# A smaller warm-up operand, and the last cast of a kernel shared by two engines

## Chip, cores, metric

The kernel runs on one core of one Trainium2 chip. The metric is the device time of one execution in microseconds (us), lower is better. A profile gives the *span*, from the first to the last instruction; here it is about 1.8 us shorter than the device time (318.9 against 320.73 us for the profiled execution of the kernel before).

## The reference

A dense layer with SiLU and its gradients, all in bf16. B=1, S=2048, D=640, F=1536.

```python
def _fwd_reference(x, w1, w2):
    h = jnp.einsum("bsd,df->bsf", x, w1)
    h = _silu(h)
    return jnp.einsum("bsf,fd->bsd", h, w2)

def reference(x, w1, w2, grad_out):          # cut: dtype plumbing
    out, vjp = jax.vjp(_fwd_reference, x, w1, w2)
    return (out, *vjp(grad_out))             # out, gx, gw1, gw2
```

## The kernel before

Two places matter: the first 8 us and the last 4.

**The start.** TensorE has nothing to do until x arrives. It fills the time with matmuls on a tile of ones, meant to have its clock released sooner: in the trace of before, the first products run 213 ns apart until the trace records the release, at 5.66 us, and 109 ns apart after it. These matmuls, and the first loads, are moved ahead of the entry barrier. Then ten PE transposes turn the first rows of x, and `h_first` multiplies them by w1, slice by slice as the slices land.

```python
warm = cpool.tile([P, P], dt_in, name="warm")
early = [nc.vector.memset(warm[:], 1.0)]
...
wp = ps_h.tile([P, SC], FP32, name="wp", tag="hp")
for i in range(NWARM):                                   # NWARM = 18
    early.append(nc.tensor.matmul(wp[:, 0:P], lhsT=warm[:], rhs=warm[:], start=True, stop=True))
...
early += [load_x(nc.sync, 0), load_x(nc.scalar, 1)]
early += [load_w1(0, slice(0, F // 2)), load_w1(0, slice(F // 2, F), nc.scalar)]
early += [load_w1(k) for k in range(1, 3)]
start_before_entry_wait(nc, {i.ins.name for i in early})
...
    # h_first: 12 products for each of the 5 slices (dt_) of w1
    for dt_ in range(DT):
        for pair in range(NPAIR):
            h_pair_mm(hs[0][pair], pair, dt_, xT, halves[0])
    for pair in range(NPAIR):
        pair_silu(hs[0][pair], pair, aT, halves[0])      # ScalarE reads hs[0][pair] in PSUM
        if pair < NCOPY:
            h_sb = hpool.tile([P, 2, HC], FP32, name="h_sb")
            nc.vector.tensor_copy(out=h_sb[:], in_=hs[0][pair][:])   # VectorE reads it too
```

**The end.** The last tile of gw1 (128x512) is computed in two PSUM banks, 384 columns and then 128. Each part is cast to bf16 and stored. Only the cast and the store of the last 128 columns come after the last matmul. `wait_for_last_store_last` makes the closing waits check this store last.

```python
for k, (lo, hi) in enumerate(((0, FC - P), (FC - P, FC))):
    gp = ps_h.tile([P, FC], FP32, name="hp")
    for st in range(ST):
        nc.tensor.matmul(gp[:, lo:hi], lhsT=x_nat[:, st, dt_ * P:(dt_ + 1) * P],
                         rhs=gh_blk[:, st, lo:hi], start=(st == 0), stop=(st == ST - 1))
    g1 = s1pool.tile([P, FC], dt_in, name="g1")          # s1pool has 3 buffers
    if k == 0:
        nc.scalar.activation(g1[:, lo:hi], gp[:, lo:hi], ACT.Copy)
    else:
        nc.vector.tensor_copy(out=g1[:, lo:hi], in_=gp[:, lo:hi])
    last_store = nc.sync.dma_start(
        out=gw1_v[:, dt_, fc * FC + lo:fc * FC + hi], in_=g1[:, lo:hi])
wait_for_last_store_last(nc, last_store.ins.name)
```

The semaphores between engines are not in the source: the framework places them where it sees a conflict between two instructions.

Of the kernel before, what the change touches and what calls it, by code (L numbers as in the profile page):

```python
# [9 lines left out]
ACT = mybir.ActivationFunctionType  # L10
# [32 lines left out]
def wait_for_last_store_last(nc, name):  # L43



    def move(nc):
        blocks = nc.m.functions[0].blocks
        store = next(i for b in blocks for i in b.instructions if i.name == name)
        lanes = {u.id for u in store.sync_info.on_update}  # L50
        end = blocks[-1].instructions
        at = next(k for k, i in enumerate(end) if i.engine == mybir.EngineType.SP)
        waits = list(end[at].sync_info.on_wait)
        late = [w for w in waits if w.id in lanes]
        assert len(late) == 1 and not end[at].sync_info.on_update
        waits = late + [w for w in waits if w.id not in lanes]
        end[at] = copy.replace(end[at], sync_info=mybir.SyncInfo(on_wait=waits, on_update=[]))

    nc.at_finalize(move)
# [3 lines left out]
def kernel(  # L63
# [11 lines left out]
    nc = tc.nc  # L75
    P = 128
# [13 lines left out]
    NFC = F // FC  # L90
    FB = FC // P
    LAG = 2
    NWARM = 18
    HC = 2 * P
    NPAIR = FT // 2
    NCOPY = 4
    dt_in = x.dtype
# [35 lines left out]
    with ExitStack() as mctx:  # L133
        cpool = mctx.enter_context(tc.tile_pool(name="cpool", bufs=1))
# [4 lines left out]
        hpool = mctx.enter_context(tc.tile_pool(name="hpool", bufs=NCOPY))  # L139
        opool = mctx.enter_context(tc.tile_pool(name="opool", bufs=2))  # L140

        warm = cpool.tile([P, P], dt_in, name="warm")
        early = [nc.vector.memset(warm[:], 1.0)]
        warm_a = cpool.tile([P, 1], FP32, name="warm_a")
        wp = ps_h.tile([P, SC], FP32, name="wp", tag="hp")
        for i in range(NWARM):
            early.append(nc.tensor.matmul(wp[:, 0:P], lhsT=warm[:], rhs=warm[:], start=True, stop=True))

        ident = cpool.tile([P, P], dt_in, name="ident")
        make_identity(nc, ident[:])  # L150
# [166 lines left out]
        for c in range(NCH):  # L317
# [15 lines left out]
            if c == 0:  # L333
                h_first(xT, aT, ghT)
                nc.sync.dma_start(
                    out=aT_scr[:, c * SC:(c + 1) * SC].rearrange("(ft p) s -> p ft s", p=P), in_=aT[:]
                )
                sd_phase(c, w2_nat, aT, oT_scr)
                for ft in range(FT):
                    g_group(ft, goT, ghT)  # L340
                nc.sync.dma_start(
                    out=ghT_scr[:, c * SC:(c + 1) * SC].rearrange("(ft p) s -> p ft s", p=P), in_=ghT[:]
# [4 lines left out]
            for i in range(FT + LAG):  # L347
# [7 lines left out]
                out=aT_scr[:, c * SC:(c + 1) * SC].rearrange("(ft p) s -> p ft s", p=P), in_=aT[:]  # L355
            )
            nc.sync.dma_start(
                out=ghT_scr[:, c * SC:(c + 1) * SC].rearrange("(ft p) s -> p ft s", p=P), in_=ghT[:]
# [7 lines left out]
    with ExitStack() as fctx:  # L366
# [18 lines left out]
        for fc in range(NFC):  # L385
            a_blk = a_blks[fc]
            g2T = fpool.tile([P, DT, FC], dt_in, name="g2T")
# [3 lines that stand above are left out]
                    nc.tensor.matmul(  # L391
                        gp[:],
                        lhsT=go_nat[:, st, dt_ * P:(dt_ + 1) * P],
                        rhs=a_blk[:, st, :],
                        start=(st == 0),
                        stop=(st == ST - 1),
# [8 lines left out]
        def store_gw2(fc):  # L405
            g2 = fpool.tile([P, FB, D], dt_in, name="g2")
            nc.sync.dma_start_transpose(out=g2[:], in_=g2T_scr[:, fc * FC:(fc + 1) * FC])
            nc.sync.dma_start(out=gw2_v[:, fc * FB:(fc + 1) * FB, :], in_=g2[:])
# [3 lines left out]
        for fc in range(NFC):  # L412
            gh_blk = gh_blks[fc]
            for dt_ in range(DT):
                if dt_ == DT // 2:
                    store_gw2(fc)
                if fc == NFC - 1 and dt_ == DT - 1:
# [3 lines that stand above are left out]
                            nc.tensor.matmul(  # L421
                                gp[:, lo:hi],
                                lhsT=x_nat[:, st, dt_ * P:(dt_ + 1) * P],
                                rhs=gh_blk[:, st, lo:hi],
                                start=(st == 0),
                                stop=(st == ST - 1),
                            )
                        g1 = s1pool.tile([P, FC], dt_in, name="g1")
                        if k == 0:
                            nc.scalar.activation(g1[:, lo:hi], gp[:, lo:hi], ACT.Copy)  # L430
                        else:
                            nc.vector.tensor_copy(out=g1[:, lo:hi], in_=gp[:, lo:hi])  # L432
                        last_store = nc.sync.dma_start(
                            out=gw1_v[:, dt_, fc * FC + lo:fc * FC + hi], in_=g1[:, lo:hi]
                        )
                    wait_for_last_store_last(nc, last_store.ins.name)
                    continue
                gp = ps_h.tile([P, FC], FP32, name="hp")
                for st in range(ST):
                    nc.tensor.matmul(  # L440
                        gp[:],
                        lhsT=x_nat[:, st, dt_ * P:(dt_ + 1) * P],
                        rhs=gh_blk[:, st, :],
                        start=(st == 0),
                        stop=(st == ST - 1),
                    )
                g1 = s1pool.tile([P, FC], dt_in, name="g1")
                if k % 2 == 0:
                    nc.scalar.activation(g1[:], gp[:], ACT.Copy)
                else:  # L450
                    nc.vector.tensor_copy(out=g1[:], in_=gp[:])  # L451
                k += 1
                nc.sync.dma_start(out=gw1_v[:, dt_, fc * FC:(fc + 1) * FC], in_=g1[:])
# [30 lines left out]
```

## Time and profile before

| | before |
|---|---|
| time, 3 runs ahead of the prediction | 320.31 us (320.27 to 320.48) |
| span of the profiled run | 318.92 us |
| TensorE busy | 314.2 us, 99% |
| end of the last matmul to the issue of the last store | 0.410 us |
| issue of the last store to its landing | 1.455 us |
| its landing to the end of the span | 0.775 us |

The profile page, busy times and the chain of waits (shares of the span by engine):

```profile
PE 314.2 (99%) x1516; PEld 150.7 (47%) x1544; DVE 102.7 (32%) x182; ACT 76.8 (24%) x139; POOL 0.7 (0%) x6
...
PE 96%; DMA 2%; issue 1%; SPq 0%; DVE 0%; DVEq 0%
```

TensorE is the bound from end to end. A change outside it can only act where TensorE does not run yet or no longer runs.

The timeline of the start. Columns: start in us, duration in us, engine, line, operation, tiles, shapes; in brackets the idle time of the engine before it and what ended it.

```profile
0.28 0.17 DVE L143 MEMSET warm<- 128x128 bf16 x1 [0.28 <-issue]
...
0.50 2.10 PE L147 MATMUL wp<-warm 128*128 128x128 bf16 x18 [0.50 <-DVE warm L143]
...
2.59 0.98 PEld L195 LDWEIGHTS <-x_nat 128*128 128x128 bf16 x10 [0.25 <-DMA x_nat<-in_x_dram]
...
6.18 1.21 PEld L233 LDWEIGHTS <-w_nat 128*128 128x128 bf16 x12 [0.30 <-DMA w_nat<-in_w_dram]
...
7.73 0.33 PEld L233 LDWEIGHTS <-w_nat 128*128 128x128 bf16 x4 [0.35 <-DMA w_nat<-in_w_dram]
```

The brackets are the point: after the warm-up, the transposes wait for x, and the products wait for two slices of w1. The chain of waits, in order of time, for the same stretch (start, duration, what), says the same:

```profile
1.47 6.22 DMA w_nat<-in_w_dram
7.69 0.05 issue
7.74 10.65 PE hp L233 x96
```

The end, as chain of waits, and the last matmul and the stores in the timeline (the second line merges two stores; the last one is the final 0.33 us of it, 316.69 to 317.02):

```profile
312.79 3.51 PE hp L421 x32
316.30 0.04 DVEq L432
316.33 0.04 issue
316.38 0.29 DVE g L432
```

```profile
316.06 0.22 PE L421 MATMUL hp<-gh_blk,x_nat 128*128 128x128 bf16 x1
...
315.94 1.08 SPq L433 DMA_DIRECT2D out_dram<-g  x2
```

A cast of 128 columns is thus in series with everything that follows. One more line is from the list of waits between 10 and 12 us: engine, tile and line, what it waited for, total us, times, longest:

```profile
DVE h_sb L266 <- ACT aT L242: 7.1, 1, 7.1
```

VectorE's copy writes `h_sb` and reads PSUM. It uses no result of ScalarE's silu, which only *reads* the same PSUM tile. Still it waited for it.

### The profile page before, as it was taken

How to read it: one execution, taken by the hardware profiler on the slowest of the kernel's cores; microseconds unless marked ns; L12 is line 12 of the kernel's file. 1: busy time of each engine (PE TensorE's matmuls, PEld its weight loads, DVE VectorE, ACT ScalarE, POOL GpSimd, SP SyncE). 2: the span in 40 equal slices, each digit the busy share in tenths (PEclk: the TensorE clock that was granted, in tenths of full speed). 3: DMA queues.
4: the chain of work that ended last, by engine and by line, in shares of the span. 5: the costliest groups of instructions: out<-in, count | busy, mean ns of one | idle time of the engine just before them, and what ended most of it. 6: DMA issues, size and time to landing. Idle time of an engine off the chain costs nothing.

```text
span 318.9 us, 3632 instructions
## 1 busy us (share of the span) xinstructions
PE 314.2 (99%) x1516; PEld 150.7 (47%) x1544; DVE 102.7 (32%) x182; ACT 76.8 (24%) x139; POOL 0.7 (0%) x6
## 2 busy tenths in 40 slices
PE   9999999999999999999999999999999999999996
PEld 7854444444444444444444444444444444444443
DVE  1494641477410187710147741000000100001001
ACT  2691000644201354311064420111100001001100
POOL 0000000000000000000000000000000000000000
PEclk9999999999999999999999999999999999999999
DMA  8999999999999866492544089919999999996111
GB/s 268 311 177 222 216 266 255 313 270 304 260 232 342 201 191 174 144 299 82 164 120 128 0 268 265 210 38 290 222 258 255 228 214 339 229 311 216 38 39 45
DMA packets 147233, 67.02 MB, mean 210 GB/s; under 512 B 113937, under 2 KB 146705, under 8 KB 147217
## 3 DMA queue, kind: packets, MB, share of 16 engines
q1 hardware_dynamic: 146928, 66.43, 83.0%
q10 hardware_dynamic: 288, 0.36, 0.3%
q8 instruction: 12, 0.20, 0.3%
q14 instruction: 5, 0.03, 0.0%
HBM read 9.18 MB, written 28.97 MB: 120 GB/s over the span
## 4 chain that ended last, share of the span: by engine, by line
PE 96%; DMA 2%; issue 1%; SPq 0%; DVE 0%; DVEq 0%
PE hp L302 32%; PE hp L286 16%; PE hp L391 16%; PE hp L440 15%; PE hp L204 12%; PE hp L233 3%; DMA w_nat<-in_w_dram 2%; PE hp L421 1%; SPq L173 0%; SPq L170 0%; DVE g L432 0%; DVEq L432 0%; SPq L468 0%
## 5 line engine op out<-in xcount | busy, mean ns | idle before, releaser
L286 PE MATMUL hp<-goT,w2T 128*128 128x512 bf16 x239 | 56.8, 379 | 0.1
L302 PE MATMUL hp<-ghT,w1T 128*128 128x512 bf16 x235 | 52.2, 379 | 0.3
L302 PE MATMUL hp<-aT,w_nat 128*128 128x512 bf16 x234 | 52.1, 379 | 0.3
L391 PE MATMUL hp<-a_blk,go_nat 128*128 128x512 bf16 x235 | 51.7, 379 | 0.3
L440 PE MATMUL hp<-gh_blk,x_nat 128*128 128x512 bf16 x219 | 48.2, 379 | 0.3
L204 PE MATMUL hp<-xT,w_nat 128*128 128x512 bf16 x174 | 43.4, 379 | 0.3
L310 ACT ACTIVATE oT<-hp 128x512 bf16<-128x512 f32 x24 | 14.5, 604 | 106.8 <-PE hp L302 106.8
L302 PEld LDWEIGHTS <-w1T 128*128 128x128 bf16 x240 | 23.5, 98 | 28.3
L391 PEld LDWEIGHTS <-go_nat 128*128 128x128 bf16 x240 | 23.5, 98 | 28.3
L286 PEld LDWEIGHTS <-w2T 128*128 128x128 bf16 x240 | 23.5, 98 | 28.3
L302 PEld LDWEIGHTS <-w_nat 128*128 128x128 bf16 x240 | 23.5, 98 | 28.1
L293 DVE SCALAR_TENSOR_TENSOR ghT<-ghT,hp 128x512 bf16<-128x512 bf16 x48 | 32.5, 681 | 7.3 <-PE hp L286 7.3
L440 PEld LDWEIGHTS <-x_nat 128*128 128x128 bf16 x224 | 21.9, 98 | 26.4
L312 DVE CAST oT<-hp 128x512 bf16<-128x512 f32 x16 | 11.1, 691 | 72.2 <-PE hp L302 67.7
L213 ACT ACTIVATE aT<-hp 128x512 bf16<-128x512 f32 x36 | 21.5, 597 | 30.4 <-PE hp L204 30.4
L204 PEld LDWEIGHTS <-w_nat 128*128 128x128 bf16 x180 | 17.6, 98 | 21.3
L220 DVE SCALAR_TENSOR_TENSOR ghT<-aT,v 128x512 bf16<-128x512 bf16 x36 | 24.6, 684 | 0.2
L219 DVE TENSOR_SCALAR v<-t 128x512 bf16<-128x512 f32 x36 | 15.4, 426 | 26.7 <-ACT t L217 26.7
L217 ACT ACTIVATE t<-hp 128x512 f32<-128x512 f32 x36 | 21.3, 592 | 0.0
L451 DVE CAST g<-hp 128x512 bf16<-128x512 f32 x7 | 4.8, 691 | 47.0 <-PE hp L440 34.5
L401 DVE CAST g2T<-hp 128x512 bf16<-128x512 f32 x7 | 4.8, 692 | 46.1 <-PE hp L391 46.1
L399 ACT ACTIVATE g2T<-hp 128x512 bf16<-128x512 f32 x8 | 4.8, 597 | 47.0 <-PE hp L391 47.0
(28 smaller groups left out, 77.3 us busy)
## 6 DMA issues: line engine op xcount, KB each, us to landing
aT_scr<-aT SPq DMA_DIRECT2D x4, 1536.0 KB, 6.3
ghT_scr<-ghT SPq DMA_DIRECT2D x4, 1536.0 KB, 8.2
out_dram<-o_sb SPq DMA_DIRECT2D x8, 640.0 KB, 3.3
oT_scr<-oT SPq DMA_DIRECT2D x4, 640.0 KB, 3.6
go_nat<-in_grad_out_dram SPq DMA_DIRECT2D x4, 640.0 KB, 8.3
gxT_scr<-oT SPq DMA_DIRECT2D x4, 640.0 KB, 4.7
w_nat<-in_w_dram SPq DMA_DIRECT2D x1, 1920.0 KB, 11.1
x_nat<-in_x_dram SPq DMA_DIRECT2D x3, 640.0 KB, 7.2
```

Of the source, the lines that this page charges most:

```text
L204: nc.tensor.matmul(hp[:], lhsT=w1_nat[:, dt_, ft * P:(ft + 1) * P], rhs=xT[:, dt_, :], start=(dt_ == 0), stop=(dt_ == DT - 1),)
L213: nc.scalar.activation(aT[:, ft, :], hp[:], ACT.Silu)
L217: nc.scalar.activation(t[:], hp[:], ACT.Tanh, scale=0.5)
L219: nc.vector.tensor_scalar(out=v[:], in0=t[:], scalar1=-0.5, scalar2=0.5, op0=ALU.mult, op1=ALU.add)
L220: nc.vector.scalar_tensor_tensor(out=ghT[:, ft, :], in0=aT[:, ft, :], scalar=1.0, in1=v[:], op0=ALU.subtract, op1=ALU.mult)
L286: nc.tensor.matmul(gp[:], lhsT=w2T[:, dt_, ft * P:(ft + 1) * P], rhs=goT[:, dt_, :], start=(dt_ == 0), stop=(dt_ == DT - 1),)
L293: nc.vector.scalar_tensor_tensor(out=ghT[:, ft, :], in0=ghT[:, ft, :], scalar=1.0, in1=gp[:], op0=ALU.add, op1=ALU.mult)
L302: nc.tensor.matmul(op_[:], lhsT=w_all[:, ft, dt_ * P:(dt_ + 1) * P], rhs=rhs_all[:, ft, :], start=(ft == 0), stop=(ft == FT - 1),)
L310: nc.scalar.activation(oT[:, dt_, :], op_[:], ACT.Copy)
L312: nc.vector.tensor_copy(out=oT[:, dt_, :], in_=op_[:])
L391: nc.tensor.matmul(gp[:], lhsT=go_nat[:, st, dt_ * P:(dt_ + 1) * P], rhs=a_blk[:, st, :], start=(st == 0), stop=(st == ST - 1),)
L440: nc.tensor.matmul(gp[:], lhsT=x_nat[:, st, dt_ * P:(dt_ + 1) * P], rhs=gh_blk[:, st, :], start=(st == 0), stop=(st == ST - 1),)
```

## The change

Intent: a smaller memset lets the warm-up start sooner, with one more warm-up matmul; and two engines share the last cast, 64 columns each, so that it takes less time. The diff, cut:

```diff
-    NWARM = 18
+    NWARM = 19
...
-        warm = cpool.tile([P, P], dt_in, name="warm")
+        warm = cpool.tile([P, 2], dt_in, name="warm")
+        warm_pp = warm[:, 0:1].to_broadcast([P, P])
...
-            early.append(nc.tensor.matmul(wp[:, 0:P], lhsT=warm[:], rhs=warm[:], start=True, stop=True))
+            early.append(nc.tensor.matmul(wp[:, 0:P], lhsT=warm_pp, rhs=warm_pp, start=True, stop=True))
...
                         else:
-                            nc.vector.tensor_copy(out=g1[:, lo:hi], in_=gp[:, lo:hi])
+                            mid = (lo + hi) // 2
+                            nc.vector.tensor_copy(out=g1[:, lo:mid], in_=gp[:, lo:mid])
+                            nc.scalar.activation(g1[:, mid:hi], gp[:, mid:hi], ACT.Copy)
```

## The prediction

> **What bounds the kernel.** TensorE: PE is busy 314.2 of 318.9 us (first part of the profile), and the chain of waits is 96% PE, 2% the landing of w1. The granted clock is full from 5.66 us on. The change touches only the two ends.
>
> **Start (timeline).** The 128x128 memset runs 0.28 to 0.44 us (165 ns); 18 warm-up matmuls, 107 ns apart, follow from 0.50 us, so the array is free at about 2.40. PE then waits for the x rows (landed 2.55); the first transpose starts at 2.59. Then w1's transfers lead: the products on its second slice start at 6.18 us (landed 6.14), on its third at 7.74 (landed 7.69), each after PE had run dry.
>
> The new memset writes 2 columns; POOL's one-column memsets take 99 ns, so I estimate 60 to 100 ns, and a warm-up that starts 65 to 105 ns earlier. The 19th matmul (107 ns) fills what was gained: the end stays near 2.40 us, before x lands. On the critical path: 0. I expect the clock's release not to depend on 0.1 us of warm-up, and reading one column for all 128 to keep the 107 ns spacing.
>
> **End (timeline).** The last matmul ends at 316.28 us; VectorE's cast of 128 columns runs 316.38 to 316.67 (290 ns); its store is issued at 316.69 and lands at 318.15; the span ends at 318.92.
>
> VectorE casts take 290 ns for 128 columns, 691 for 512: 1.04 ns per column, so an estimated 223 ns for 64. ScalarE: 490 ns for 384, 597 for 512: an estimated 222 ns for 64. Side by side the halves would save about 65 ns.
>
> I expect them not to run side by side. Both read the same PSUM bank. The Trainium skill, page "PSUM — Partial Sum Buffer", section "PSUM bank collisions raise a hardware error", says that ScalarE and VectorE reads of one bank collide even at disjoint columns, and that they must be ordered by semaphores. This trace agrees that the program is so ordered: in h_first, VectorE's copy of hp to h_sb needs nothing that ScalarE writes, yet the list of waits shows it 7.1 us idle until ScalarE's silu of the same hp had ended; it began 33 ns after (11.384 to 11.417 us). So ScalarE's half should start after VectorE's: 223 ns, a handover of 30 to 80, 222 ns: about 490 ns in place of 290. The store goes out 0.2 us later, and all behind it moves too.
>
> **Predicted.** 320.31 + 0.0 (start) + 0.2 (end) = 320.5 us, span about 319.1; 8 in 10 between 320.2 and 320.9. Faster by over 2%: 0.5%; within 2%: 99%; slower by over 2%: 0.5%. A little slower rather than faster: 80%.
>
> **What would show it.** Right: ScalarE's half starts 30 to 80 ns after the end of VectorE's, released by it; last store issued about 0.6 us after the last matmul's end in place of 0.41; first transpose still at 2.59 us, waiting for x; the third slice's products still at 7.7. Wrong: the halves overlap and the store goes out about 0.35 us after the last matmul (then 320.25); or warm-up matmuls more than 107 ns apart.
>
> **What would make it wrong.** Halves not ordered; ScalarE's short cast costing more than its slope says; a slower read of the broadcast column, pushing the transposes past 2.59 us; the clock's release falling elsewhere, which could move the start by some tenths; the spread between runs (0.2 us in before), as large as the effect.

## The result, and the profile after

Six runs each, in the same rounds: 320.90 us with the change (320.64 to 321.24), 320.53 before (320.27 to 321.48). The ratio is 1.0008, with a 95% interval of 0.9994 to 1.0022. A ratio here is the mean time of one kernel's fast runs over that of the other's of the same rounds, so not quite the ratio of the two medians. The sign is not settled by these times. The traces settle what the times can't.

The chain of waits at the end, with the change; then the last matmul, ScalarE's half and the stores in the timeline:

```profile
312.86 3.51 PE hp L422 x32
316.37 0.04 DVEq L434
316.41 0.04 issue
316.45 0.23 DVE g L434
316.68 0.02 issue
316.71 0.22 ACT g L435
```

```profile
316.14 0.22 PE L422 MATMUL hp<-gh_blk,x_nat 128*128 128x128 bf16 x1
...
316.71 0.22 ACT L435 ACTIVATE g<-hp 128x64 bf16<-128x64 f32 x1 [0.72 <-DVE g L434]
...
316.02 1.27 SPq L436 DMA_DIRECT2D out_dram<-g  x2
```

The two halves stand one after the other in the chain, and the bracket names VectorE's half as what ScalarE waited for. To the ns: the last matmul ends at 316.356, VectorE's half runs 316.449 to 316.673, ScalarE's 316.706 to 316.929, the store is issued at 316.955. From matmul to store that is 0.599 us in place of 0.410.

The start, with the change, timeline and then chain of waits:

```profile
0.26 0.06 DVE L144 MEMSET warm<- 128x2 bf16 x1 [0.26 <-issue]
...
0.38 2.20 PE L148 MATMUL wp<-warm 128*128 128x128 bf16 x19 [0.38 <-DVE warm L144]
...
2.58 0.99 PEld L196 LDWEIGHTS <-x_nat 128*128 128x128 bf16 x10 [0.26 <-DMA x_nat<-in_x_dram]
...
3.99 5.02 PEld L234 LDWEIGHTS <-w_nat 128*128 128x128 bf16 x36 [0.43 <-DMA w_nat<-in_w_dram]
```

```profile
0.54 3.41 DMA w_nat<-in_w_dram
3.95 0.05 issue
4.00 14.47 PE hp L234 x120
```

The warm-up starts 0.12 us sooner, the last warm-up matmul 0.015 us sooner, and the transposes wait for x as before. But the chain is another one: it follows the *first* slice of w1 and then TensorE without a stop.

The whole difference of the two spans, from the traces (ns):

| stretch | before | after | difference |
|---|---|---|---|
| span's start to the first matmul of the out phase (`sd_phase`) | 18,229 | 18,304 | +75 |
| from there to the end of the last matmul | 298,053 | 298,052 | -1 |
| last matmul to issue of the last store | 410 | 599 | +189 |
| store to landing, landing to end | 2,230 | 2,224 | -6 |
| span | 318,922 | 319,179 | +257 |

Two terms are left to explain: +189 at the end, and +75 at the start, which the prediction had as 0.

### The profile page after: what moved, and what is told of

It reads as the page before. It is cut to its first block, busy times and chain, and to the rows that moved or that the text cites. A ratio compares the mean times of both kernels' runs of the same rounds, so it can differ in the third digit from the quotient of the medians.

```text
span 319.2 us, 3664 instructions
## 1 busy us (share of the span) xinstructions
PE 315.8 (99%) x1545; PEld 151.2 (47%) x1545; DVE 102.6 (32%) x182; ACT 77.0 (24%) x140; POOL 0.7 (0%) x6
## 4 chain that ended last, share of the span: by engine, by line
PE 98%; DMA 1%; SPq 0%; issue 0%; DVE 0%; ACT 0%; DVEq 0%
PE hp L303 32%; PE hp L287 16%; PE hp L392 16%; PE hp L443 15%; PE hp L205 12%; PE hp L234 5%; PE hp L422 1%; DMA w_nat<-in_w_dram 1%; SPq L171 0%; DVE g L434 0%; ACT g L435 0%; DVEq L434 0%; SPq L471 0%
```

## Experiments

Theory: the end loses 0.19 us because the two reads of one PSUM bank are ordered, and the start's part of the change is worth nothing; what differs at the start varies from run to run. Rivals: the start's part does harm; at the end, the shared *output* tile orders the halves, not the bank. (Each PSUM tile in question has a bank to itself, so "bank" below means this tile too: no run tells the two apart.)

### Each part alone, both again, and before against itself

Four kernels in the same rounds on one chip, five rounds. `a1_start_only` has the warm-up part of the diff only, `a2_end_only` the cast part only, `a3_both_again` is the change, `a4_before_again` the kernel before.

> Only the warm-up part of the change. My theory (the whole difference comes from the casts at the end; the start is worth nothing): the memset takes about 60 ns and the warm-up starts about 0.12 us earlier, but the first transpose still starts at 2.58 to 2.60 us, when x lands; last matmul to last store 0.41 us as in before; time equal to before within 0.1 us. Rival (the broadcast column or the 19th matmul puts off the release of the clock or the first products): 0.1 us or more over before, and a release of the clock near 6.5 us rather than 5.7.

> Only the split cast of the change. My theory: all of the loss is here. Last matmul's end to last store 0.60 us against 0.41, ScalarE's half 33 ns after VectorE's ends; time 0.19 us over before (0.06%). Rival (the start causes it): equal to before within 0.05 us.

> The whole change again, in the same rounds. My theory: equal to the split cast alone within 0.1 us, 0.2 us over before; the clock's release and the first products fall at other times than in the first profile of the change (they vary from run to run). Rival: the sum of both parts is 0.3 us or more, and the release is again near 6.5 us.

> The kernel before against itself: the measure of the noise, and a second sample of its start. Ratio 1.000 within 0.0005. My theory that the clock's release varies between executions of one kernel: it falls elsewhere than at 5.66 us by some tenths. Rival that it is fixed to the kernel: again at 5.6 to 5.7 us.

| | median us (lowest to highest) | ratio to before, 95% | last matmul to last store, ns | its start stretch, ns |
|---|---|---|---|---|
| before, 11 runs | 320.94 (320.46 to 321.45) | | | |
| a1_start_only | 320.74 (320.64 to 321.12) | 0.9998 (0.9986 to 1.0010) | 411 | 18,273 |
| a2_end_only | 320.82 (320.26 to 321.25) | 0.9997 (0.9984 to 1.0010) | 601 | 17,610 |
| a3_both_again | 321.34 (320.48 to 321.72) | 1.0010 (0.9996 to 1.0024) | 602 | 17,831 |
| a4_before_again | 320.74 (320.46 to 321.48) | 0.9999 (0.9986 to 1.0012) | 411 | 18,178 |

The times decide nothing: eleven runs of one kernel spread over 1 us, five times the effect. My expectations of the times (equal to 0.1 us, 0.19 us over) could not be tested at this size; `a2_end_only` even had a median below before. `a4_before_again` did come within 0.0005, but with an interval wider than that. The traces do decide the end: 0.41 us with the old cast, 0.60 with the split one, whatever the start does, and the stretch between is 298,052 or 298,053 ns in all four. My estimate in advance for `a3_both_again`, equal to `a2_end_only` within 0.1 us, was missed in the medians (0.5 us apart) though their ends agree to 1 ns. Its median even lies 0.40 us over before, as its rival said (0.3 or more), but the interval of the ratio contains 1. In `a1_start_only` the first transpose started at 2.65 us, later than expected (2.58 to 2.60), because x landed later, at 2.60.

### What makes the start vary

The same four traces, the two of the first comparison and those of the later runs, all in us. "Clock" is the time when the trace records the release of TensorE's clock, from half to full; with a ~, it has no such record and I read it from where the spacing of the matmuls halves. The first three rows have the warm-up of the change.

| run | second slice of w1 lands | third slice lands | clock | first matmul of the out phase |
|---|---|---|---|---|
| after | 5.93 | 7.26 | 6.48 | 18.30 |
| a1_start_only | 6.43 | 7.45 | 6.29 | 18.27 |
| a3_both_again | 5.99 | 6.96 | ~3.5 | 17.83 |
| before | 6.14 | 7.69 | 5.66 | 18.23 |
| a2_end_only | 5.76 | 7.05 | 4.52 | 17.61 |
| a4_before_again | 6.33 | 7.28 | 5.02 | 18.18 |
| b4_scalar_last | 5.86 | 7.57 | 5.04 | 18.11 |
| c2_scalar_fresh | 6.66 | 7.59 | ~4.0 | 18.51 |
| b3_fresh_tile | 7.01 | 7.93 | ~4.3 | 18.86 |
| b2_two_banks | 7.21 | 8.16 | 5.75 | 19.06 |
| b1_two_tiles | 6.41 | 7.55 | 9.92 | 20.49 |
| c1_no_warm | 7.14 | 8.10 | 6.60 | 19.28 |

In nine of the twelve, the last column is the landing of the second slice plus 11.847 us (seven rows) or of the third plus 10.537 (`before` and `b4_scalar_last`), each time to within 2 ns: 10.537 us is what TensorE needs from the third slice on at 109 ns per product, and the second slice has 12 products more. In `c1_no_warm` the chain of waits ends the stretch with the landing of w2 at 19.23 us. The other two are late by the clock. In `after`, the products on the first slice were 213 ns apart, half speed, until 6.48 us; the second slice had been there for 0.59 us when TensorE came to it. So that start was 0.53 us later than 5.925 + 11.847 = 17.77 us. In `b1_two_tiles`, the timeline shows TensorE idle in the middle of the first slice:

```profile
3.90 1.44 PE L233 MATMUL hp<-xT,w_nat 128*128 128x256 bf16 x6
6.26 5.98 PE L233 MATMUL hp<-xT,w_nat 128*128 128x256 bf16 x37 [0.92 <-DMA w_nat<-in_w_dram]
```

The clock then stayed at half until 9.92 us, the products 213 ns apart until then, and the start took 20.49 us. That kernel does not differ from before in its first 300 us. The record of the clock fits this: in the eight other traces that have one, the full clock lasts 314,026 ns from its release to its end after the last matmul, to the ns, and in `b1_two_tiles` 310,613 ns, which is 3,413 ns less. Both are whole multiples of 3,413 ns (92 and 91), as if the clock changed only on a grid of such steps; on that grid `b1_two_tiles` missed the step at 6.51 us, just after its wait.

So the 75 ns of the first comparison are the difference of two draws: the second slice of w1 came 0.2 us earlier than in the trace of before (the third 0.4) and the clock 0.8 us later. `a4_before_again` bore out that the release moves within one kernel: 5.02 us in place of 5.66. The rival, that the new warm-up puts the clock off, is not supported: with it the release came at 3.5, 6.3 and 6.5 us, without it at 4.0 to 9.9. Three draws are few, and a shift of the mean by some tenths stays open.

### What the whole warm-up is worth

```diff
-    NWARM = 18
+    NWARM = 1
```

> Kernel before with 1 warm-up matmul in place of 18: what the whole warm-up is worth, as an upper bound for 0.12 us more of it. My theory: the clock is released later by about 2 us on the mean, and of that what is not hidden behind w1's transfers is lost: 0.3 to 1.2 us slower. The change's 0.12 us would then be worth at most 0.12/2.0 of it, 0.02 to 0.07 us. Rival (w1's transfers hide the clock's release): within 0.2 us of before, and the warm-up is worth nothing here.

Three rounds, on another chip: 321.60 us (321.17 to 321.92) against 321.21 (320.51 to 322.59, 11 runs), ratio 1.0004 (0.9976 to 1.0033). The measured times fit both sides. In its one trace the clock was released at 6.60 us, later than in every run with the full warm-up but one (`b1_two_tiles`, 9.92), and the second slice of w1 landed last (7.14 us), after the products on the first were done. That trace fits the rival: on the first products nothing was lost. The experiment did not resolve what 18 warm-up matmuls are worth; 0.12 us more of them is, all the more, below what can be seen here.

### Which shared thing orders the two halves

First, the split cast with an output tile and a store for each half, the PSUM bank still shared (the edit against the change, cut):

```diff
+                            g1b = s1pool.tile([P, FC], dt_in, name="g1b")
                             nc.vector.tensor_copy(out=g1[:, lo:mid], in_=gp[:, lo:mid])
-                            nc.scalar.activation(g1[:, mid:hi], gp[:, mid:hi], ACT.Copy)
+                            nc.scalar.activation(g1b[:, mid:hi], gp[:, mid:hi], ACT.Copy)
+                            # and one store for each half
```

> Split cast as in the change, but each half writes an SBUF tile of its own and is stored by itself; both still read one PSUM bank. My theory (the shared PSUM bank orders the halves): ScalarE's half still starts about 33 ns after the end of VectorE's, 0.35 us after the last matmul. Rival (the shared output tile orders them): it starts 0.04 to 0.10 us after the last matmul, side by side with VectorE's. The last store is late in both (about 0.73 us after the last matmul), because the first half's store takes 332 ns to issue; only the start of ScalarE's half tells.

One look (323.37 us beside 322.72 for before, one run each, state unknown; the start in its trace, told above, is 2.3 us later than in the trace of before; the single run beside it left no trace to compare with). The timeline of its end:

```profile
318.63 0.23 DVE L437 CAST g<-hp 128x64 bf16<-128x64 f32 x1 [2.80 <-PE hp L421]
...
318.89 0.22 ACT L438 ACTIVATE g1b<-hp 128x64 bf16<-128x64 f32 x1 [0.72 <-DVE g L437]
```

ScalarE still waits for VectorE and starts 34 ns after its end, 351 ns after the last matmul (350 with the change). The output tile is not what orders them. The last store went out 770 ns after the last matmul, as nearly expected (0.73), since it waits for the first half's issue.

Second, the other way round: one output tile, but two groups of 64 columns in two PSUM banks, their matmuls alternating (cut):

```diff
-                                nc.tensor.matmul(gp[:, lo:hi], ...)
+                            for gp, c0, c1 in gps:      # two PSUM tiles of 64 columns
+                                nc.tensor.matmul(gp[:, c0:c1], ...)
...
-                            nc.vector.tensor_copy(out=g1[:, lo:hi], in_=gp[:, lo:hi])
+                            nc.vector.tensor_copy(out=g1[:, lo:mid], in_=gps[0][0][:, lo:mid])
+                            nc.scalar.activation(g1[:, mid:hi], gps[1][0][:, mid:hi], ACT.Copy)
```

> The last 128 columns accumulated as two groups of 64 in two PSUM banks, their matmuls alternating, so that both groups end within one matmul; casts to one SBUF tile, one store. My theory (bank): the casts overlap, and the store follows the last matmul by about 0.35 us (93 + 224 + 27 ns), 0.06 less than in before; the 16 added matmuls cost 16 x (twice the spacing of a 64-column matmul less 56 ns): nothing at 28 ns, 0.9 us at 56 ns, so the span tells their spacing. Rival (shared output tile): ScalarE's half starts 33 ns after VectorE's, and the store follows by 0.6 us.

```profile
317.21 0.22 DVE L436 CAST g<-hp 128x64 bf16<-128x64 f32 x1 [2.81 <-PE hp L425]
317.24 0.22 ACT L437 ACTIVATE g<-hp 128x64 bf16<-128x64 f32 x1 [0.50 <-PE hp L425]
317.50 0.33 SPq L438 DMA_DIRECT2D out_dram<-g  x1
```

Now each half waits for TensorE alone, and they run side by side, 29 ns apart. The store follows the last matmul by 349 ns. The 64-column matmuls are 29 ns apart, so the 16 added ones cost 16 x (2 x 29.2 - 55.8) = 41 ns by the spacings, and the stretch up to the last matmul is 298,094 ns, 41 over the usual. Net: 349 + 41 = 390 against 410 ns. So sharing the cast can pay, by 20 ns, once the halves lie in two banks. (Its one run took 321.52 us beside 322.72 for before, state unknown; the start decides such single times, so I read nothing from them.)

A reason for such an order is in the Trainium skill, page "PSUM — Partial Sum Buffer", section "PSUM bank collisions raise a hardware error": ScalarE and VectorE reading one bank at once collide, at disjoint columns too, and software must prevent it. The runs show the order, and that it comes with the shared PSUM bank and not with the shared output tile. They do not show the collision, since no kernel without the wait was run: that part rests on the page.

### What else stands between matmul and cast

VectorE's cast starts 93 ns after the end of the last matmul, but the first copies of the kernel start 38 ns after theirs. In the chain of before, a separate wait instruction (DVEq L432) stands in between: the cast waits for TensorE and also for ScalarE, whose output was in that buffer three tiles ago, and for the store that emptied it. Given a buffer that nobody used earlier:

```diff
-                        g1 = s1pool.tile([P, FC], dt_in, name="g1")
+                        g1 = s1pool.tile([P, FC], dt_in, name="g1", tag="g1" if k == 0 else "g1_last")
```

> Kernel before, but the last cast writes a tile of which nobody used the buffer earlier, so VectorE has no wait for ScalarE or for old stores there. My theory: of the 93 ns between the last matmul and the cast, about 55 are a separate wait instruction of VectorE, passed only when the last matmul is done; without it the cast starts 38 ns after the matmul, like the first copy of the kernel (38 ns after the transposes), and the store goes out 0.35 us after in place of 0.41. Rival: 93 ns are VectorE's latency from PSUM; nothing changes (0.41).

```profile
316.69 0.22 PE L421 MATMUL hp<-gh_blk,x_nat 128*128 128x128 bf16 x1
...
316.94 0.29 DVE L432 CAST g<-hp 128x128 bf16<-128x128 f32 x1 [2.75 <-PE hp L421]
```

Measured: the cast starts 38 ns after the last matmul, the store goes out after 357 ns. As expected; 55 ns were the wait instruction, not VectorE's latency.

Then the engines exchanged:

```diff
-                        if k == 0:
+                        if k == 1:
                             nc.scalar.activation(g1[:, lo:hi], gp[:, lo:hi], ACT.Copy)
```

> Kernel before with the two engines of the last tile exchanged: VectorE casts the first 384 columns, ScalarE all of the last 128. From ScalarE's 490 ns for 384 and 597 for 512 columns I estimate 276 ns for 128; it started 36 ns after its matmul in before. My theory: store 0.34 us after the last matmul if ScalarE's wait for the matmul is on the cast itself, 0.40 if it is on a separate wait instruction. Rival (ScalarE is dearer on short casts than its slope says): over 0.41.

Measured: ScalarE's cast of 128 columns takes 277 ns (276 estimated) and starts after 86 ns; store after 389 ns. That is the branch "separate wait instruction" (0.40).

### Both steps together

```diff
-                        g1 = s1pool.tile([P, FC], dt_in, name="g1")
-                        if k == 0:
+                        g1 = s1pool.tile([P, FC], dt_in, name="g1", tag="g1" if k == 0 else "g1_last")
+                        if k == 1:
                             nc.scalar.activation(g1[:, lo:hi], gp[:, lo:hi], ACT.Copy)
```

> What the runs so far point to: ScalarE casts the last 128 columns into a tile whose buffer nobody used before, VectorE the 384 before. Sum of the two single steps: 36 ns after the last matmul, 277 ns, 26 ns: store 0.34 us after the last matmul in place of 0.41 (0.60 in the change). Everything else as before, so 0.07 us less, 0.02%: I expect the profile to show it and the times (spread 0.3 us and more) not to.

```profile
316.34 0.22 PE L421 MATMUL hp<-gh_blk,x_nat 128*128 128x128 bf16 x1
...
316.60 0.28 ACT L430 ACTIVATE g<-hp 128x128 bf16<-128x128 f32 x1 [6.35 <-PE hp L421]
...
316.29 0.94 SPq L433 DMA_DIRECT2D out_dram<-g  x2
```

The cast starts 37 ns after the last matmul, takes 278 ns, and the store is issued 340 ns after the matmul: 70 ns less than before and 259 less than the change. The times, 320.99 us (320.61 to 321.39, 6 runs) against 321.21 (11 runs), ratio 0.9990 (0.9970 to 1.0010), can't show 70 ns. It is the best end of all that I ran, by its trace alone.

## Why the prediction was right, and where not

- **End, +0.2 us: right, mechanism and size.** Estimated 223 ns + 30 to 80 + 222 ns; measured 224 + 33 + 223. From matmul to store 0.599 us for "about 0.6". That the shared bank is the cause was argued from one wait in the trace of before, and from the page; `b1_two_tiles` and `b2_two_banks` showed it (bank and PSUM tile being one here).
- **Warm-up, off the critical path: right in what it named.** The memset took 60 ns, the warm-up began 0.12 us earlier (I had said 0.065 to 0.105), the spacing stayed at 107 ns with the broadcast column, and the first transpose waited for x at 2.58 us.
- **"the third slice's products still at 7.7": wrong.** They began at 7.82 us, and did not wait for w1. I took one trace's order of events, clock first and w1 last, for a property of the kernel. It is one draw; in the trace of the change the clock came at 6.48 us and TensorE was the later one. I had named this risk (the release "could move the start by some tenths"), and that draw lost 0.53 us by it.
- **The size of the whole: right with luck.** 320.9 us lies on the edge of the range, because the runs of before in the same rounds were at 320.53, not 320.31. Between these medians lie 0.37 us, of which the end accounts for 0.19; the rest is of the size of the spread. That three runs agreed within 0.2 us had made me think the spread smaller than the 1 us and more that 11 runs showed.

## What to carry to other kernels

Splitting a cast between two engines shortened it here only when the halves lay in different PSUM banks; in one bank they were ordered, and two fixed costs (about 157 and 170 ns) ran in series. For the last instruction of a kernel, look at what it waits for beside its data: a fresh buffer took away 55 ns that looked like latency. And where an effect is below the spread of the times, cut the span of each trace at the points where the variation enters, and compare the stretches: here two of three stretches repeat to a few ns.

## What the Trainium skill lacked or had wrong

- "TensorE: Matmul & The Clock Gate", section "Back-to-back issue gap": gives a sustained spacing of about 81 ns for 128 columns and 131 ns for 512 in streams of weight load and matmul. Here such streams ran at 56 and 216 ns, the values that the page gives for an isolated gap. Its table has about 60 cycles (25 ns) for 1 to 64 columns; 64 columns took 29 ns, which the formula above that table gives.
- The same page, section "Part 1: The HAM clock gate (the "warmup" mystery)": says that the window is free-running and the number of slow matmuls varies. The runs agree and add the size: release between about 3.5 and 9.9 us after the start for the same 18 or 19 warm-up matmuls. They agree with its length of the window too, 3,413 ns: by so much did the full clock of `b1_two_tiles` last less than in eight other traces (310,613 against 314,026 ns). There TensorE had waited 0.92 us for data before the release (one case, so that the wait put it off is not shown). The page does not say how short a wait within the window does that.
- "Perfetto Trace Analysis", section "Optimizing Scalar/DVE Operations": gives access overheads for PSUM of about 125 ns (VectorE) and 51 ns (ScalarE), and twice that as profiled latency. The profiled casts from PSUM took 224, 291, 558 and 691 ns on VectorE and 223, 277, 491 and 597 ns on ScalarE for 64, 128, 384 and 512 columns: a fixed part of about 157 and 170 ns, so ScalarE's is not the smaller one.
- The same page, section "Identifying Dependency Chains", says that instructions with several waits may get separate wait instructions. It lacks the cost: about 50 to 55 ns when the last event is behind the separate one (93 against 38 ns on VectorE, 86 against 37 on ScalarE).
- "PSUM — Partial Sum Buffer": the order that its rule on banks asks for was found here, and no page says what it costs: a handover of 33 ns between the two engines, beside the serial casts.
